# Queries and keys transposed unsplit, and scores as half-height products of two heads

## The chip, the core and the metric

The kernel runs on one core of a Trainium2 chip. The metric is the device time of one execution in microseconds (us), the median of several runs. The engines are named as in the profile: PE (matmul; PEld is its weight load), DVE (vector), ACT (scalar), POOL (GpSimd) and SP, whose queue issues every transfer here.

## The reference

Windowed attention with a distance bias, then a feed-forward layer with a rational activation. All is float32. Sizes: 4 batches, 8 heads, 768 positions, 64 dimensions a head; 8 global and 96 local positions; the feed-forward layer has 3072 tokens, 512 by 2048 weights.

```python
scores = scale * np.matmul(q, k.transpose(0, 1, 3, 2))
is_global = pos[None, :] < int(n_global)
is_local = (rel >= 0) & (rel < int(n_local))
keep = is_global | is_local
scores = scores + bias[None, :, :, :]          # -slope of the head * distance
scores = np.where(keep, scores, -1000000000.0)
a = np.exp(scores - np.max(scores, axis=-1, keepdims=True))
a = a / (np.sum(a, axis=-1, keepdims=True) + 1e-09)
x = np.matmul(a, v)                            # to [3072, 512]
h = x @ w_in
g = (a0 + a1*h + a2*h*h + a3*h*h*h) / (1 + |b0|*|h| + |b1|*h*h + 1e-6)
out = g @ w_out
```

## The kernel before

The 3072 tokens are 24 blocks of 128 positions (i is the block's number in its batch, 0 to 5). A unit u is one block with two neighbouring heads (p is the pair of heads), so there are 96 units; two units that follow each other share a load of q, k and v for four heads. Here m = u // 2 numbers these. A chunk is two blocks, 256 tokens: 8 units of attention and 8 steps f of the feed-forward layer.

The float32 products run in one of two ways. In one, a number is split into a high part, rounded to the type float32r (`FR`), and the low rest, and a product becomes three products of these parts of float32r operands; in the other it stays one product of plain float32 operands. The feed-forward layer after the first chunk goes the first way, with weights and activations split: `st_ffn1` (line 257, output `h`, 256 columns) and `st_ffn2` (line 333, output `acc`, 512 columns). In the first chunk both run on plain float32 (lines 249 and 328), while the weights are still being loaded, decoded (lines 162 to 191; some bit work on DVE, ACT and POOL) and split (lines 208, 209).

Attention, for one unit, in stages:

- `st_load` (lines 131 to 134): three transfers bring q and k of four heads into `nat`, v into `vt`.
- `st_split` (368, 369): DVE rounds q and k of two heads to float32r, POOL subtracts to get the low part; both lie side by side in `sp`, 64 columns high and 64 low for each head.
- `st_qkT` (377): four transposes on PE. For each head the result `tk` has the 64 high rows above the 64 low rows.
- `st_qkE` (391 to 396): ACT brings q (times a power of two that belongs to the head) into `qT` and k into `kT`. Two transfers on SP (392, 393) make a second copy of q in which the high and low halves of the partitions have changed places. `kT` keeps two blocks of keys per head, the block's own and the one before; `kG` keeps the first 8 keys, which line 409 copies into the older block.
- `st_score` (407, output `s`): two products per head over all 128 rows, one with `qT` and one with the exchanged copy, so that all four products of high and low parts are summed. DVE (418) adds the mask, scales and takes the minimum of each row.
- `st_soft` (428 to 433): ACT takes the exponential, DVE adds up and inverts. `st_norm` (440): POOL scales the probabilities.
- `st_pT` (450, output `tp`): PE transposes the probabilities. For each pair of units, `st_pv` (467, output `o`) multiplies with v, each head into 64 of the 128 output columns, and `st_x` (486, 487) splits the result into `xh` and `xl` for the feed-forward layer.

PSUM has two buffers for `h`, two for `acc`, one for the activation and three, tagged `t`, that `tk`, `s`, `tp` and `o` share in turn.

One loop over t calls all stages; each call gets a priority from t and a table (`PRI`, `PRI_A` for the first chunk), and a scheduler orders the instructions of every engine from these priorities and from its own simulated timeline. Attention runs 12 units ahead of the feed-forward layer (`LAG`). Each engine then takes its own instructions in that fixed order, and so does the queue of SP.

A second path for other window sizes (`general`) is compiled in, but with these inputs it isn't taken.

Of the kernel before, what the change touches and what calls it, by code (L numbers as in the profile page):

```python
# [94 lines left out]
def tile_kernel(ctx: ExitStack, tc: tile.TileContext, q, k, v, n_global, n_local,  # L95
# [126 lines left out]
    stats = const.tile([P, 4, 8], F32, name="stats")  # L222

    def load_coef():
        nc.sync.dma_start(out=coef[:, 0:4], in_=ca.partition_broadcast(P))
# [122 lines left out]
    ident = const.tile([P, P], F32, name="ident")  # L350
# [13 lines left out]
    def st_split(u):
        p = unit(u)[2]
        n = nat[u // 2][:, :, 2 * (p % 2):2 * (p % 2) + 2, :]
        s = pl.att.tile([P, 2, 2, 2, D], FR, tag="split", name=f"sp{u}", bufs=1)
        nc.vector.tensor_copy(out=s[:, :, :, 0, :], in_=n)  # L368
        nc.gpsimd.tensor_tensor(out=s[:, :, :, 1, :], in0=n, in1=s[:, :, :, 0, :], op=ALU.subtract)  # L369
        sp[u] = s  # L370

    def st_qkT(u):
        s = sp.pop(u)
        tk = pl.ps_t.tile([P, 2, 2, P], FR, tag="t", name=f"tk{u}")
        for z in range(2):
            for x in range(2):
                nc.tensor.transpose(out=tk[:, z, x, :], in_=s[:, z, x].rearrange("p a d -> p (a d)"),  # L377
                                    identity=ident_r)
        tqk[u] = tk

    def st_qkE(u):
        c, t, p, b, i = unit(u)
        tk = tqk.pop(u)
        hs = slice(2 * p, 2 * p + 2)
        qT = pl.att.tile([P, 2, 2, P], FR, tag="qT", name=f"qT{u}", bufs=3)
        for x in range(2):

            nc.scalar.activation(out=qT[:, 0, x], in_=tk[:, 0, x], func=AF.Copy, scale=float(2.0 ** (2 * p + x - 2)))
        nc.sync.dma_start(out=qT[0:D, 1].bitcast(F32), in_=qT[D:P, 0].bitcast(F32))
        nc.sync.dma_start(out=qT[D:P, 1].bitcast(F32), in_=qT[0:D, 0].bitcast(F32))
        nc.scalar.copy(out=kT[:, hs, i % 2, :], in_=tk[:, 1])
        if i == 0:
            nc.scalar.copy(out=kG[:, hs, :], in_=tk[:, 1, :, 0:G])
        qTs[u] = qT

    def st_score(u):
        c, t, p, b, i = unit(u)  # L400
        qT = qTs.pop(u)
        s_ps = pl.ps_t.tile([P, 2, 2, P], F32, tag="t", name=f"s{u}")
        for x in range(2):
            h = 2 * p + x
            rhs = kT[:, h] if i else kT[:, h, 0:1, :].broadcast_to([P, 2, P])
            for z in range(2):
                nc.tensor.matmul(out=s_ps[:, x], lhsT=qT[:, z, x, :], rhs=rhs, start=(z == 0), stop=(z == 1))  # L407
        if 1 <= i < NT - 1:
            nc.gpsimd.tensor_copy(out=kT[:, 2 * p:2 * p + 2, i % 2, 0:G], in_=kG[:, 2 * p:2 * p + 2, :])
        if i == 0:  # L410
            mk = mask0
        else:
            mk = masks[:, 0:2, :] if i % 2 else masks[:, 1:3, :]
        pr = pl.att.tile([P, 2, 2, P], F32, tag="prob", name=f"pr{u}")
        st = stats[:, u % 4]
        for x in range(2):
            h = 2 * p + x
            nc.vector.tensor_tensor_reduce(  # L418
                out=blocks_of(pr[:, x], i), in0=blocks_of(s_ps[:, x], i), in1=mk,
                scale=-(2.0 ** -(h + 1)), scalar=3e38, op0=ALU.add, op1=ALU.min, accum_out=st[:, x:x + 1])  # L420
        prob[u] = (pr, st)

    def st_soft(u):
        i = unit(u)[4]
        pr, st = prob[u]
        for x in range(2):
            d = blocks_of(pr[:, x], i)
            nc.scalar.activation(out=d, in_=d, func=AF.Exp, scale=-1.0, bias=st[:, x:x + 1],  # L428
                                 accum_out=st[:, 2 + 2 * x:3 + 2 * x])

        nc.vector.tensor_reduce(out=st[:, 6:8], in_=st[:, 2:6].rearrange("p (x w) -> p x w", w=2), op=ALU.add,
                                axis=mybir.AxisListType.X)
        nc.vector.reciprocal(out=st[:, 6:8], in_=st[:, 6:8])  # L433

    def st_norm(u):
        i = unit(u)[4]
        pr, st = prob[u]
        for x in range(2):
            d = blocks_of(pr[:, x], i)
            nc.gpsimd.tensor_scalar(  # L440
                out=d, in0=d, scalar1=st[:, 6 + x:7 + x], scalar2=None, op0=ALU.mult)
# [51 lines left out]
    def windowed():  # L493
# [217 lines left out]
```

## Time and profile before

| | |
|---|---|
| median of 3 runs | 793.19 us (793.1 to 794.15) |
| the profiled execution | 793.47 us, of which its span is 791.7 us |
| busy, PE / PEld | 745.0 us (94%) / 647.2 us (82%) |
| busy, DVE / ACT / POOL | 589.6 us (74%) / 573.0 us (72%) / 531.7 us (67%) |
| matmuls | 5184 records |
| granted PE clock, mean | 0.996 |

The span runs from the first to the last instruction. In the rows of the profile a name like `s<-kT,qT` is output and inputs by the program's names, `L407` the line, `128*64 128x128` the part of the array used (rows by columns of weights) and the size of the output. A plain float32 product with no transpose leaves two records in the trace. Rows of matmuls overlap, since they are pipelined: what one costs the next is the distance between their starts. A group's row ends with the idle time of its engine ahead of it and what ended that. Stretches are given in us from the start of the span.

### The profile page before, as it was taken

The numbers are of one execution on the slowest core, as the hardware profiler recorded it, in microseconds if no ns is written. First come the engines' busy times: TensorE is split into PE (matmuls) and PEld (weight loads), VectorE is DVE, ScalarE is ACT, GpSimd is POOL, SyncE is SP. The second block draws the span as 40 slices with busy tenths as digits, with TensorE's granted clock in tenths as the row PEclk, the third lists the DMA queues.
The fourth block names the chain that finished last, engine by engine and source line by source line (L and its number), as shares of the span: only waits on it lengthen the run. The fifth ranks groups of instructions, "written<-read, shape, count | busy, mean of one in ns | idle before, by whom it ended". The sixth has DMA issues, their size and how long they took to land.

```text
span 791.7 us, 15480 instructions
## 1 busy us (share of the span) xinstructions
PE 745.0 (94%) x5184; PEld 647.2 (82%) x5184; DVE 589.6 (74%) x1453; ACT 573.0 (72%) x1407; POOL 531.7 (67%) x572
## 2 busy tenths in 40 slices
PE   3678998899999999999999999999999999999995
PEld 2466656598988998988998988988998988988993
DVE  5899998988786767776776767776776767776664
ACT  4688767776786777777777777777777777776763
POOL 3887657998966676675676676675677676664440
PEclk9999999999999999999999999999999999999999
DMA  7884555122121222222222222222222222100000
GB/s 182 233 228 144 158 156 159 44 65 64 43 58 23 62 55 49 62 54 58 57 47 49 61 55 48 61 55 53 63 48 48 61 56 48 41 15 1 27 1 32
DMA packets 101400, 55.90 MB, mean 71 GB/s; under 512 B 81856, under 2 KB 94144, under 8 KB 101312
## 3 DMA queue, kind: packets, MB, share of 16 engines
q1 hardware_dynamic: 101312, 54.82, 26.3%
q8 instruction: 44, 0.72, 0.4%
q14 instruction: 44, 0.36, 0.1%
HBM read 35.92 MB, written 6.29 MB: 53 GB/s over the span
## 4 chain that ended last, share of the span: by engine, by line
PE 81%; DVE 9%; POOL 3%; DMA 2%; issue 2%; ACT 1%; SPq 0%; DVEq 0%; POOLq 0%; ACTq 0%
PE h L257 32%; PE acc L333 30%; PE s L407 5%; PE o L467 5%; PE tp L450 4%; PE tk L377 3%; POOL pr L440 2%; PE acc L328 1%; DMA qT<-qT 1%; DVE pr L418 1%; DMA r<-in_moe_w_out_dram 1%; DVE fu L304 1%; POOL sp L369 1%; DVE fu L288 1%; DVE r L189 1%
## 5 line engine op out<-in xcount | busy, mean ns | idle before, releaser
L333 PE MATMUL acc<-wout_h,g 128*128 128x512 f32 x704 | 250.1, 406 | 0.8 <-ACT g L312 0.8
L257 PE MATMUL h<-xh,win_h 128*128 128x256 f32 x704 | 204.7, 291 | 2.4 <-DVE fu L289 2.4
L440 POOL TENSOR_SCALAR pr<-pr,stats 128x256 f32<-128x256 f32 (+1 forms) x192 | 180.5, 950 | 32.9 <-DVE stats L433 15.5
L257 PE MATMUL h<-xl,win_h 128*128 128x256 f32 x704 | 197.7, 281 | 0.0
L290 POOL TENSOR_TENSOR fa<-fa,fs 128x512 f32<-128x512 f32 x95 | 124.5, 1311 | 91.1 <-ACT fs L283 87.3
L333 PEld LDWEIGHTS acc<-wout_h,g 128*128 128x128 f32 x704 | 128.5, 188 | 23.3 <-ACT g L312 1.2
L257 PEld LDWEIGHTS h<-xh,win_h 128*128 128x128 f32 x704 | 132.5, 188 | 11.3 <-issue 6.6
L369 POOL TENSOR_TENSOR sp<-nat,sp 128x256 fp32r<-128x256 f32 x96 | 75.9, 791 | 95.8 <-DVE sp L368 45.8
L257 PEld LDWEIGHTS h<-xl,win_h 128*128 128x128 f32 x704 | 132.4, 188 | 1.8 <-issue 0.5
L428 ACT ACTIVATE pr<-pr,stats 128x256 f32<-128x256 f32 (+1 forms) x192 | 92.6, 485 | 55.2 <-DVE stats L418 55.0
L281 ACT ACTIVATE fu<-h,coef 128x512 f32<-128x512 f32 (+1 forms) x97 | 75.0, 774 | 60.3 <-PE h L257 59.4
L313 POOL TENSOR_TENSOR g<-fu,g 128x512 fp32r<-128x512 f32 x87 | 112.7, 1295 | 7.9 <-DVE fu L289 4.5
L302 DVE SCALAR_TENSOR_TENSOR fu<-fu,coef,q 128x512 f32<-128x512 f32 (+1 forms) x97 | 71.6, 738 | 48.2 <-ACT q L298 47.2
L297 ACT ACTIVATE fs<-fa,coef 128x512 f32<-128x512 f32 (+1 forms) x97 | 69.6, 718 | 34.9 <-POOL fa L290 32.5
L452 DVE COPY pT<-tp 128x512 f32<-128x512 f32 (+1 forms) x75 | 48.5, 646 | 61.8 <-PE tp L450 61.2
L288 DVE TENSOR_TENSOR fu<-fu,h 128x512 f32<-128x512 f32 (+1 forms) x97 | 65.3, 673 | 12.3 <-ACT fs L283 10.7
L407 PE MATMUL s<-kT,qT 128*128 128x256 f32 x384 | 70.2, 304 | 4.4 <-DMA qT<-qT 3.4
L289 DVE SCALAR_TENSOR_TENSOR fu<-fu,coef,h 128x512 f32<-128x512 f32 (+1 forms) x97 | 71.8, 740 | 2.6
L450 PE MATMUL tp<-ident,pr 128*128 128x128 f32 x352 | 63.0, 282 | 10.7 <-POOL pr L440 10.2
L303 DVE SCALAR_TENSOR_TENSOR q<-fa,coef,q 128x512 f32<-128x512 f32 (+1 forms) x97 | 72.1, 743 | 0.0
L407 PEld LDWEIGHTS s<-kT,qT 128*128 128x128 f32 x384 | 60.4, 199 | 11.6 <-issue 2.4
L283 ACT ACTIVATE fs<-h,coef 128x512 f32<-128x512 f32 (+1 forms) x97 | 66.5, 685 | 0.1
(271 smaller groups left out, 1622.5 us busy)
## 6 DMA issues: line engine op xcount, KB each, us to landing
qT<-qT SPq DMA_DIRECT2D x192, 64.0 KB, 2.1
r<-in_moe_w_in_dram SPq DMA_DIRECT2D x16, 512.0 KB, 5.4
r<-in_moe_w_out_dram SPq DMA_DIRECT2D x16, 512.0 KB, 3.5
nat<-in_q_dram SPq DMA_DIRECT2D x48, 128.0 KB, 2.7
nat<-in_k_dram SPq DMA_DIRECT2D x48, 128.0 KB, 2.5
vt<-in_v_dram SPq DMA_DIRECT2D x48, 128.0 KB, 2.3
out_dram<-o SPq DMA_DIRECT2D x24, 256.0 KB, 2.1
vt<-in_v_dram SPq DMA_DIRECT2D x32, 8.0 KB
```

What stands on the lines that cost most here:

```text
L257: nc.tensor.matmul(out=hps[f][:, y, :], lhsT=w[:, fs], rhs=x[:, ct, :], start=(n == 0), stop=(n == 3 * NCT - 1))
L281: nc.scalar.activation(out=u, in_=h, func=AF.Identity, scale=a3, bias=a2)
L288: nc.vector.tensor_tensor(out=u, in0=u, in1=h, op=ALU.mult)
L290: side(f).tensor_tensor(out=a, in0=a, in1=s, op=ALU.add)
L303: nc.vector.scalar_tensor_tensor(out=r, in0=a, scalar=q1, in1=r, op0=ALU.add, op1=ALU.mult)
L313: side(f).tensor_tensor(out=g[:, 1, ys], in0=u, in1=g[:, 0, ys], op=ALU.subtract)
L333: nc.tensor.matmul(out=acc, lhsT=gs[f][:, z, y, ts], rhs=w, start=(ft == 0 and n == 0), stop=(ft == NFT - 1 and n == 2))
L369: nc.gpsimd.tensor_tensor(out=s[:, :, :, 1, :], in0=n, in1=s[:, :, :, 0, :], op=ALU.subtract)
L407: nc.tensor.matmul(out=s_ps[:, x], lhsT=qT[:, z, x, :], rhs=rhs, start=(z == 0), stop=(z == 1))
L428: nc.scalar.activation(out=d, in_=d, func=AF.Exp, scale=-1.0, bias=st[:, x:x + 1], accum_out=st[:, 2 + 2 * x:3 + 2 * x])
L440: nc.gpsimd.tensor_scalar(out=d, in0=d, scalar1=st[:, 6 + x:7 + x], scalar2=None, op0=ALU.mult)
L450: nc.tensor.transpose(out=t_ps[:, x, w, :], in_=pr[:, x, w, :], identity=ident)
```

## The change

q and k are no longer split ahead of the transposes. They are loaded into a new tile `natf`, and a transfer within SBUF copies them to `nat`, which has the type float32r: the bits stay as they are, without rounding. PE transposes these for two pairs of heads at once: `tk` of one m holds q of both pairs and k of both pairs, where a pair's two heads have 64 rows each. The split is made on the way out of PSUM: ACT rounds to the high parts, DVE subtracts to get the low parts. `qT` and `kT` now hold high and low parts in separate planes, with one head of a pair in rows 0 to 63 and the other in rows 64 to 127; the exchanged copy and its two transfers are gone. A score is three products (high by high, high by low, low by high) over 64 rows; the two heads of a pair write two different `t` buffers, and the source issues their products in turn. `qkT`, `qkE`, `score` and `soft` run once per m, on all four heads; the first eight keys are copied by POOL.

```diff
-        n = pl.ldp.tile([P, 2, 4, D], F32, tag="nat", name=f"nat{u}")
-        nc.sync.dma_start(out=n[:, 0], in_=q[b, hs, r, :].rearrange("h s d -> s h d"))
-        nc.sync.dma_start(out=n[:, 1], in_=k[b, hs, r, :].rearrange("h s d -> s h d"))
+        nf = pl.ldp.tile([P, 2, 4, D], F32, tag="natf", name=f"natf{u}", bufs=1)
+        n = pl.ldp.tile([P, 2, 4, D], FR, tag="nat", name=f"nat{u}")
+        nc.sync.dma_start(out=nf[:, 0], in_=q[b, hs, r, :].rearrange("h s d -> s h d"))
+        nc.sync.dma_start(out=nf[:, 1], in_=k[b, hs, r, :].rearrange("h s d -> s h d"))
+        nc.sync.dma_start(out=n.bitcast(F32), in_=nf)
...
+    def st_qkT(m):
+        n = nat[m]
+        tk = pl.ps_t.tile([P, 2, 2, P], FR, tag="t", name=f"tk{m}")
         for z in range(2):
+            for y in range(2):
+                nc.tensor.transpose(out=tk[:, z, y, :], in_=n[:, z, 2 * y:2 * y + 2, :].rearrange("p a d -> p (a d)"),
+                                    identity=ident_r)
+        tqk[m] = tk.bitcast(F32)
+
+    def st_qkE(m):
+        p, i = of_pairs(m)
+        tk = tqk.pop(m)
+        qT = qTs[m] = pl.att.tile([P, 2, 2, P], FR, tag="qT", name=f"qT{m}")
+        kh, kl = (kT[:, p:p + 2, z, i % 2, :] for z in range(2))
+        for y in range(2):
+            nc.scalar.activation(out=qT[:, 0, y], in_=tk[:, 0, y], func=AF.Identity, scale=qs[:, p + y:p + y + 1])
+        nc.scalar.copy(out=kh, in_=tk[:, 1])
+        for y in range(2):
+            nc.vector.scalar_tensor_tensor(out=qT[:, 1, y], in0=tk[:, 0, y], scalar=qs[:, p + y:p + y + 1],
+                                           in1=qT[:, 0, y], op0=ALU.mult, op1=ALU.subtract)
+        nc.vector.tensor_tensor(out=kl, in0=tk[:, 1], in1=kh, op=ALU.subtract)
+        if i == 0:
+            nc.gpsimd.tensor_copy(out=kG[:, p:p + 2], in_=kT[:, p:p + 2, :, 0, 0:G])
+
+    def st_score(m):
+        p, i = of_pairs(m)
+        qT = qTs.pop(m)
+        sx = [pl.ps_t.tile([P, 2, 2, P], F32, tag="t", name=f"s{x}_{m}") for x in range(2)]
+        for y in range(2):
+            for n, (zq, zk) in enumerate(((0, 0), (0, 1), (1, 0))):
+                for x in range(2):
+                    r = slice(x * D, (x + 1) * D)
+                    nc.tensor.matmul(out=blocks_of(sx[x][:, y], i), lhsT=qT[r, zq, y, :],
+                                     rhs=blocks_of(kT[r, p + y, zk], i), start=(n == 0), stop=(n == 2))
...
-            on("score", st_score, t - 2)
-            on("soft", st_soft, t - 2)
+                on_m("score", st_score, m - 1)
+                on_m("soft", st_soft, m - 1)
             on("ffn1a", st_ffn1, f, 0)
-            on("qkT", st_qkT, t)
-            if t % 2:
-                on("pv", lambda u: st_pv(u // 2), t - 5)
-            on("qkE", st_qkE, t)
-            if t % 2:
-                on("x", lambda u: st_x(u // 2), t - 5)
-            if t:
-                on("split", st_split, t + 1)
+            if odd:
+                on_m("qkT", st_qkT, m)
+                on_m("pv", st_pv, m - 2)
+                on_m("qkE", st_qkE, m)
+                on_m("x", st_x, m - 2)
```

More of the change, by code (lines that the diff above doesn't have):

```diff
@@ L221, in tile_kernel @@
     a0, a1, a2, a3, b0, _, b1, q1 = (coef[:, x:x + 1] for x in range(8))
-    stats = const.tile([P, 4, 8], F32, name="stats")
+    stats = const.tile([P, 4, 16], F32, name="stats")
     def load_coef():
@@ L342, in st_ffn2 @@
             nc.sync.dma_start(out=out[rows, :], in_=o)
-    kT = const.tile([P, H, 2, P], FR, name="kT")
-    kG = const.tile([P, H, G], FR, name="kG")
+    kT = const.tile([P, NPAIR, 2, 2, P], FR, name="kT")
+    kG = const.tile([P, NPAIR, 2, G], FR, name="kG")
     ident = const.tile([P, P], F32, name="ident")
     ident_r = const.tile([P, P], FR, name="ident_r")
+    qs = const.tile([P, NPAIR], F32, name="qs")
     mask0 = const.tile([P, P], F32, name="mask0")
     masks = const.tile([P, 3, P], F32, name="masks")
-    sp = {}
+    qTs = {}
     tqk = {}
-    qTs = {}
     prob = {}
@@ L362, in blocks_of @@
         return x if i else x[..., 0, :]
[L364 to L374, printed above, removed]
-        for z in range(2):
-            for x in range(2):
-                nc.tensor.transpose(out=tk[:, z, x, :], in_=s[:, z, x].rearrange("p a d -> p (a d)"),
-                                    identity=ident_r)
-        tqk[u] = tk
@@ L384, in st_qkE @@
[L384 to L388, printed above, removed]
-        for x in range(2):
[L391 to L441, printed above, removed]
+    def of_pairs(m):
+        c, t, p, b, i = unit(2 * m)
+        return p, i
+    def st_qkT(m):
+        n = nat[m]
+        tk = pl.ps_t.tile([P, 2, 2, P], FR, tag="t", name=f"tk{m}")
+        for z in range(2):
+            for y in range(2):
+                nc.tensor.transpose(out=tk[:, z, y, :], in_=n[:, z, 2 * y:2 * y + 2, :].rearrange("p a d -> p (a d)"),
+                                    identity=ident_r)
+        tqk[m] = tk.bitcast(F32)
@@ new lines, in st_score @@
+    def st_score(m):
[8 more added lines that the diff above has]
+                                     rhs=blocks_of(kT[r, p + y, zk], i), start=(n == 0), stop=(n == 2))
+        if 1 <= i < NT - 1:
+            nc.gpsimd.tensor_copy(out=kT[:, p:p + 2, :, i % 2, 0:G], in_=kG[:, p:p + 2])
+        mk = mask0 if i == 0 else masks[:, 0:2, :] if i % 2 else masks[:, 1:3, :]
+        st = stats[:, m % 4]
+        for y in range(2):
+            u = 2 * m + y
+            prob[u] = pl.att.tile([P, 2, 2, P], F32, tag="prob", name=f"pr{u}", bufs=3)
+            for x in range(2):
+                nc.vector.tensor_tensor_reduce(
+                    out=blocks_of(prob[u][:, x], i), in0=blocks_of(sx[x][:, y], i), in1=mk,
+                    scale=-(2.0 ** -(2 * (p + y) + x + 1)), scalar=3e38, op0=ALU.add, op1=ALU.min,
+                    accum_out=st[:, 2 * y + x:2 * y + x + 1])
@@ new lines, in st_soft @@
+    def st_soft(m):
+        i = of_pairs(m)[1]
+        st = stats[:, m % 4]
+        for n in range(4):
+            d = blocks_of(prob[2 * m + n // 2][:, n % 2], i)
+            nc.scalar.activation(out=d, in_=d, func=AF.Exp, scale=-1.0, bias=st[:, n:n + 1],
+                                 accum_out=st[:, 4 + 2 * n:5 + 2 * n])
+        nc.vector.tensor_reduce(out=st[:, 12:16], in_=st[:, 4:12].rearrange("p (x w) -> p x w", w=2), op=ALU.add,
+                                axis=mybir.AxisListType.X)
+        nc.vector.reciprocal(out=st[:, 12:16], in_=st[:, 12:16])
@@ L443, in st_pT, with st_norm @@
+    def st_norm(u):
+        m, y = divmod(u, 2)
+        i = of_pairs(m)[1]
+        for x in range(2):
+            d = blocks_of(prob[u][:, x], i)
+            nc.gpsimd.tensor_scalar(out=d, in0=d, scalar1=stats[:, m % 4, 12 + 2 * y + x:13 + 2 * y + x],
+                                    scalar2=None, op0=ALU.mult)
     def st_pT(u):
         i = unit(u)[4]
-        pr, st = prob.pop(u)
+        pr = prob.pop(u)
         W = 2 if i else 1
@@ L499, in windowed @@
         nc.vector.tensor_copy(out=ident_r, in_=ident)
+        for p in range(NPAIR):
+            for x in range(2):
+                nc.gpsimd.memset(qs[x * D:(x + 1) * D, p:p + 1], 2.0 ** (2 * p + x - 2))
         nc.vector.tensor_copy(out=nf, in_=ni)
         load_coef()
-        st_split(0)
-        st_split(1)
         nl, ng = nf[:, 0:1], nf[:, 2:3]
```

7 lines of the change are left out of this document (6 added, 1 removed).

## The prediction

> **What bounds the kernel now.** I read the busy time by stretch first, then who waits for whom on TensorE, then single stretches of its timeline, then the groups by line, and the chain of the opening last. The four stretches (columns: window, length, then busy time and instructions of PE, PEld, DVE, ACT, POOL, granted clock, DMA share, GB/s):
>
> ```profile
> 0.00:20.00 20.00, 7.04 (x34) 5.82 (x34) 11.52 (x59) 9.13 (x35) 6.94 (x18) 1.00 0.73 184
> 20.00:160.00 140.00, 116.23 (x649) 82.87 (x649) 131.78 (x323) 105.57 (x272) 107.87 (x108) 0.99 0.56 161
> 160.00:740.00 580.00, 579.44 (x4256) 522.02 (x4255) 417.99 (x1027) 429.09 (x1051) 400.28 (x435) 1.00 0.20 49
> 740.00:791.70 51.70, 42.31 (x251) 36.52 (x249) 28.31 (x47) 29.24 (x52) 16.59 (x13) 0.97 0.06 23
> ```
>
> From 160 to 740 us PE is covered for 579.44 of 580 us, while DVE, ACT and POOL are at 69 to 74%. Before that, DVE is the full one: 131.78 of 140 us. Cover alone does not prove that PE sets the pace, since each matmul's row includes its way through the pipe; its waits do, from 160 us on:
>
> ```profile
> PE h L257 <- DVE fu L289: 1.8, 1, 1.8
> PE acc L333 <- ACT g L312: 0.8, 1, 0.8
> PE s L407 <- ACT kT L394: 0.6, 1, 0.6
> ```
>
> So 3.2 us of waits in 630. In this stretch a step added to PE's queue is a step added to the time, and work taken from DVE, ACT or POOL is worth nothing. I therefore cost PE by start-to-start steps, not by durations. The timeline of PE (start, length, instruction) at one block of four transposes `tk`:
>
> ```profile
> 407.56 0.28 PE L257 MATMUL h<-xh,w_2l 128*128 128x256 f32 x1
> 407.68 0.46 PE L377 MATMUL tk<-ident_r,sp 128*128 128x128 f32 x4
> 407.98 0.35 PE L257 MATMUL h<-xh,win_h 128*128 128x256 f32 x1
> 408.16 0.29 PE L257 MATMUL h<-xl,win_h 128*128 128x256 f32 x1
> ```
>
> A 256-column product steps by 0.12 us (407.56 to 407.68; a row further down gives 0.118). The block and the product behind it take 408.16 - 407.68 = 0.48 us, so the block costs 0.36 us. Four scores, next:
>
> ```profile
> 404.14 0.66 PE L407 MATMUL s<-kT,qT 128*128 128x256 f32 x4
> 404.63 0.40 PE L333 MATMUL acc<-wout_h,g 128*128 128x512 f32 x1
> ```
>
> 0.49 us, some 0.12 each. Then `o` (L467), the only products here that do not use the whole array (128 rows by 64 columns, the two heads alternating), in a run of 16 records and one of 8; each of its products leaves two records:
>
> ```profile
> 712.10 0.28 PE L257 MATMUL h<-xh,w_2l 128*128 128x256 f32 x1
> 712.31 1.09 PE L467 MATMUL o<-pT,vt 128*64 128x128 f32 x16
> 713.33 0.38 PE L257 MATMUL h<-xh,win_h 128*128 128x256 f32 x1
> 713.55 0.28 PE L257 MATMUL h<-xl,win_h 128*128 128x256 f32 x1
> ...
> 714.73 0.28 PE L257 MATMUL h<-xh,w_2l 128*128 128x256 f32 x1
> ...
> 386.31 0.66 PE L467 MATMUL o<-pT,vt 128*64 128x128 f32 x8
> 386.89 0.38 PE L257 MATMUL h<-xh,win_h 128*128 128x256 f32 x1
> ...
> 95.79 3.69 PE L249 MATMUL h<-x,w_2f 128*128 128x256 f32 x16
> 99.41 0.43 PE L467 MATMUL o<-pT,vt 128*64 128x128 f32 x2
> ```
>
> From 713.55 to 714.73 are ten L257 steps: 0.118 each. Eight more records of `o` take (713.33 - 712.31) - (386.89 - 386.31) = 0.44 us, 0.055 each. L249, of the same type and on the whole array, takes (99.41 - 95.79) / 16 = 0.226 us for 256 columns, 0.113 for 128: twice as much, so in `o` two halves of the array run side by side. But there is a fixed price. From 712.10 to 713.55 are 1.45 us; two L257 steps (0.236) and 16 records (0.88) leave 0.33 to 0.34 us. Of it 0.09 shows ahead of the run (712.10 to 712.31), 0.10 behind the first product after it (713.33 to 713.55), the rest inside. One run of `o` thus costs 0.34 us beyond its work.
>
> **What the order does.** An m is two units, that is, four heads of one 128-row block. The names: `s` score, `tk` transposed q and k, `o` output of attention, `tp` transposed probabilities, `acc` and `h` the two FFN products. PE at the scores, before (one unit):
>
> ```order
> L333 MATMUL acc_1_6563<-wout_h,g_6442 128x512 x2
> L333 MATMUL acc_1_6563<-w_1l,g_6442 128x512
> L333 MATMUL acc_1_6563<-wout_h,g_6442 128x512
> L407 MATMUL s_6570<-kT,qT_6403 128x256 x4
> L257 MATMUL h_6582<-xh_5603,win_h 128x256
> ```
>
> PE at the scores of m = 30, now (`s_30_5284` is the first head of each pair, rows 0 to 63; `s_30_5285` the second, rows 64 to 127):
>
> ```order
> L448 MATMUL tp_5261<-ident,pr_5105 128x128 x4
> L407 MATMUL s_30_5284<-kT,qT_5209 128x256 x6
> L335 MATMUL acc_0_4609<-wout_h,g_5058 128x512 x2
> L335 MATMUL acc_0_4609<-w_13l,g_5058 128x512
> L335 MATMUL acc_0_4609<-wout_h,g_5058 128x512
> L335 MATMUL acc_1_4621<-wout_h,g_5058 128x512 x2
> L335 MATMUL acc_1_4621<-w_13l,g_5058 128x512
> L335 MATMUL acc_1_4621<-wout_h,g_5058 128x512
> L407 MATMUL s_30_5285<-kT,qT_5209 128x256 x6
> ```
>
> The source writes the two heads in turn, but the six products of one stand apart from the six of the other: the second score tile gets its PSUM buffer later. PE at `o`, before:
>
> ```order
> L377 MATMUL tk_6595<-ident_r,sp_6514 128x128 x4
> L467 MATMUL o_6600<-pT_6462,vt_5670 64x128 x2
> L467 MATMUL o_6600<-pT_6462,vt_5264 64x128 x2
> L467 MATMUL o_6600<-pT_6561,vt_5670 64x128 x2
> L467 MATMUL o_6600<-pT_6561,vt_5264 64x128 x2
> L257 MATMUL h_6582<-xh_5603,win_h 128x256
> ```
>
> and now:
>
> ```order
> L378 MATMUL tk_5576<-ident_r,nat_5084 128x128 x4
> L465 MATMUL o_5581<-pT_5457,vt_4716 64x128 x2
> L465 MATMUL o_5581<-pT_5457,vt_4351 64x128 x2
> L259 MATMUL h_5563<-xh_4471,win_h 128x256
> L259 MATMUL h_5563<-xl_4472,win_h 128x256
> L259 MATMUL h_5563<-xh_4471,w_0_2l 128x256
> L259 MATMUL h_5563<-xh_4471,win_h 128x256
> L259 MATMUL h_5563<-xl_4472,win_h 128x256
> L465 MATMUL o_5581<-pT_5555,vt_4716 64x128 x2
> L465 MATMUL o_5581<-pT_5555,vt_4351 64x128 x2
> ```
>
> One run of `o` has become two. The trace of before starts its matmuls in the compiled order. Counted over it from the first split FFN product on (near 160 us): before, 37.5 m with 300 scores, 43 runs of `o`; now 39 m with 468 scores in 68 runs, 78 runs of `o`. Of the 468, 72 have 128 columns, and 67 stand right behind one of the other head without a partner yet. I take 38 m for the full stretch.
>
> **The sum, PE, per m.**
> 1. Transposes: one block of four instead of two. -0.36.
> 2. Scores: 12 products instead of 8. At 0.118 each, 1.42 against 0.94. The 128-column ones step by 0.07 (a `tk` block has four in 0.30), which saves 1.85 x 0.05 = 0.09; partners side by side, as in `o`, save 1.7 x 0.11 = 0.19. Net +0.19. Without any overlap it is +0.38.
> 3. Runs of `o`: 2.0 instead of 1.15, at 0.34. +0.29.
> 4. Runs of half-height products: 1.74, where there were none. No row shows one. The lower bound is 0. The upper is the price of `o`, 0.34, with a full weight load in place of a half one at both edges, 0.05 each (rows below: 188 against 136 ns): 0.44. Nearest is `o`, also a product on part of the array; I add the wider load at the entry alone: 0.39. +0.68.
>
> ```profile
> L407 PEld LDWEIGHTS s<-kT,qT 128*128 128x128 f32 x291 | 44.1, 188 | 6.0 <-ACT kT L394 0.8
> L467 PEld LDWEIGHTS o<-pT,vt 128*64 128x64 f32 x560 | 30.3, 136 | 3.8 <-issue 0.6
> ```
>
> Ends: +4 with term 4 at 0, +40 with 0.44 and no overlap in term 2. Together +0.80 us per m, times 38: +30. Term 4 is 26 of it. The Trainium skill, page "TensorEngine Tiling (Array Packing)", section "Tiling Modes", says that a change of tiling mode, not merely of tile, drains TensorE. The rows of `o` agree for columns (0.34 us a run); no run here shows rows yet. By that rule the sum is the +30 above; without it, +4.
>
> **The other engines, per m.** Their rows from 160 to 740 us:
>
> ```profile
> L369 POOL TENSOR_TENSOR sp<-nat,sp 128x256 fp32r<-128x256 f32 x71 | 52.6, 740 | 77.7 <-DVE stats L431 33.8 <-DVE sp L368 33.3 <-DVE stats L433 6.6
> L368 DVE CAST sp<-nat 128x256 fp32r<-128x256 f32 x70 | 25.5, 365 | 34.8 <-POOL kT L409 13.7 <-PE tk L377 8.9 <-POOL g L313 7.1
> L487 DVE TENSOR_TENSOR xl<-o,xh 128x256 fp32r<-128x256 f32 x38 | 15.9, 417 | 3.1 <-ACT xh L486 3.1
> L418 DVE CUSTOM_DVE_ANT_0 pr<-s,mask 128x128 f32<-128x128 f32 x24 | 6.0, 284 | 0.2
> L433 DVE RECIPROCAL stats<-stats 128x2 f32<-128x2 f32 x73 | 11.6, 159 | 1.0
> L431 DVE TENSOR_REDUCE stats<-stats 128x2 f32<-128x4 f32 x73 | 11.1, 152 | 10.1 <-ACT pr L428 10.0
> L391 ACT ACTIVATE qT<-tk 128x128 fp32r<-128x128 f32 x144 | 30.4, 262 | 3.0 <-PE tk L377 2.9
> L394 ACT CAST kT<-tk 128x256 fp32r<-128x256 f32 x72 | 26.6, 369 | 0.0
> ```
>
> POOL loses two subtractions, -1.48 us. ACT loses half of its evictions, 2 x 262 + 369, -0.89. DVE loses two casts (0.73) and one pair of reduce and reciprocal (0.31); it gains three subtractions out of PSUM, 2 x 0.284 + 0.417 by the nearest rows: -0.05. POOL has eight small fills more at the start. In the full stretch all of this is slack.
>
> On SP, four transfers of the two halves of `qT` go and one inside SBUF comes, which waits for both loads and for the transposes of the m two earlier; behind it stand the loads of v and the stores of results. `qT` took 2.1 us to land (issue row: `qT<-qT`, 64 KB). The data are wanted two m later, some 28 us, so I cost it at nothing there. At the very start nothing covers it.
>
> The opening, to 165 us, by the chain of what ended last:
>
> ```profile
> by line: issue 8.6%; POOL pr L440 7.4%; PE acc L328 6.7%; DMA qT<-qT 3.7%; DVE pr L418 3.7%; DMA r<-in_moe_w_out_dram 3.6%; PE h L257 3.4%; POOL sp L369 3.1%; DVE r L189 3.0%; DMA r<-in_moe_w_in_dram 3.0%; PE s L407 3.0%; PE tk L377 2.8%; D
> ```
>
> `qT` and `sp`, which go, are 6.8% of 165 us: 11 us at most. The low end is -11. The high end is +5, two landings in a row before the first transposes. DVE, nearly full there, hardly loses work, so I take -4.
>
> The profiled execution took 793.5 us, against the median of 793.2: 793.5 + 30 - 4 = 820 us.
>
> **The rivals.**
> - *Half-height runs cost nothing* (term 4 is 0). For it: the scores keep all 128 columns, and the measured price is one of split columns. Against it: in `o` the price sits at both edges, as a pipe that empties would. 794 us with my opening, 787 with its low end. This is the case on the faster side: it ends below 791.6 if a run costs under 0.07 us and the opening gives its 11.
> - *PSUM buffers become the wait.* Scores now hold two of the three `t` buffers at once, and `tk`, `tp` and `o` need the third. For it: the heads torn apart above. Against it: of the PE waits above at most the 0.6 us of `s` for ACT can be a `t` buffer, and tiles per m fall from 7 to 6. At half a us per m: +19, 839 us.
> - *Weight loads within a half no longer hide.* Each of the 8.6 products per m without a partner of the other half would add its 0.188: +61, 881 us. Against it: L407 loads 0.188 us for every 0.118 step on one set of rows. The Trainium skill, "TensorE: Matmul & The Clock Gate", Part 3, says that weight loads overlap running matmuls only when the row group differs; those rows contradict it for the full array.
>
> **How the numbers follow.** 0.68 for 820, 0.20 for free runs, 0.07 for PSUM, 0.05 for weight loads. A measurement here can tell about 0.2%, 1.6 us. Free runs split into 0.10 faster, 0.05 same, 0.05 slower; the rest is slower: 0.85. The range leaves out about a tenth below (free runs with a short opening) and the weight loads with half of the PSUM case above: 792 to 842.
>
> **What would show it.** `tk` rows halve to 192. The L407 rows read 64*128. At the edges of their runs PE steps some 0.2 us, as at `o`; if they step 0.12, term 4 is wrong. Inside a run of one head steps stay at 0.12, and a pair of two heads starts within 0.01 us. Between 160 us and the last score PE stays covered, with waits of a few us; waits of `s`, `tk` or `tp` for DVE or ACT of over 10 us mean the PSUM rival. POOL's busy time falls by some 70 us, without use.

## The result, and the profile after

The changed kernel takes 829.05 us (median of 4 runs, 826.8 to 830.16), the kernel before 793.67 us on the same chip (4 runs): ratio 1.044, interval 1.0414 to 1.0467. The profiled execution took 829.64 us, its span is 827.8 us: 36.1 us more than before. The prediction said 820 us, between 792 and 842.

Busy time by stretch (columns as in the prediction; the last stretch again begins some 52 us ahead of the end):

```profile
0.00:20.00 20.00, 3.72 (x21) 2.74 (x21) 10.79 (x57) 8.14 (x24) 5.11 (x22) 1.00 0.71 202
20.00:160.00 140.00, 114.99 (x585) 79.68 (x586) 123.63 (x289) 90.55 (x218) 80.41 (x78) 0.94 0.51 154
160.00:776.00 616.00, 615.33 (x4330) 527.59 (x4329) 426.18 (x1016) 423.19 (x955) 345.97 (x349) 1.00 0.17 47
776.00:827.80 51.80, 42.56 (x252) 36.78 (x250) 28.57 (x47) 29.52 (x52) 16.60 (x13) 0.97 0.07 23
```

PE is covered for 615.33 of 616 us, and the other engines have become emptier. Who PE waits for from 160 us on:

```profile
PE h L259 <- DVE fu L291: 1.8, 1, 1.8
PE acc L335 <- ACT g L314: 0.8, 1, 0.8
PE s L407 <- ACT pT L450: 0.7, 1, 0.7
```

3.3 us, as before. So the time of the full stretch lies in PE's own steps. Its timeline at two runs of six scores (one head each), then at a run of twelve (the heads in turn):

```profile
550.39 0.40 PE L335 MATMUL acc<-w_2l,g 128*128 128x512 f32 x1
550.72 0.97 PE L407 MATMUL s<-kT,qT 64*128 64x256 f32 x6
551.62 0.39 PE L259 MATMUL h<-xh,win_h 128*128 128x256 f32 x1
551.84 0.28 PE L259 MATMUL h<-xl,win_h 128*128 128x256 f32 x1
552.05 0.97 PE L407 MATMUL s<-kT,qT 64*128 64x256 f32 x6
552.95 0.39 PE L259 MATMUL h<-xh,w_2l 128*128 128x256 f32 x1
553.17 0.28 PE L259 MATMUL h<-xh,win_h 128*128 128x256 f32 x1
...
441.39 0.28 PE L259 MATMUL h<-xh,win_h 128*128 128x256 f32 x1
441.60 0.99 PE L407 MATMUL s<-kT,qT 64*128 64x256 f32 x12
442.51 0.39 PE L259 MATMUL h<-xl,win_h 128*128 128x256 f32 x1
442.74 0.28 PE L259 MATMUL h<-xh,w_3l 128*128 128x256 f32 x1
```

Into the second run the step is 0.21 us (551.84 to 552.05), out of it 0.22 (552.95 to 553.17), where `h` steps by 0.118 elsewhere. From 551.84 to 553.17 are 1.33 us; less two steps of `h` (0.236) that is 1.09 us for six products, whose own steps are 6 x 0.118 = 0.71: one run costs 0.39 us beyond its work (the median of ten such runs with `h` on both sides is 1.098 us). The run of twelve takes 442.74 - 441.39 - 0.236 = 1.11 us: twelve products of two heads in turn cost what six of one head do.

The instructions by line, over the whole span:

```profile
L407 PE MATMUL s<-kT,qT 64*128 64x256 f32 x480 | 61.1, 307 | 0.7 <-ACT pT L450 0.7
L407 PE MATMUL s<-kT,qT 64*128 64x128 f32 x96 | 14.2, 319 | 1.7 <-ACT kT L389 1.0 <-DVE fl L669 0.6
L378 PE MATMUL tk<-ident_r,nat 128*128 128x128 f32 x192 | 26.0, 261 | 21.2 <-DMA nat<-natf 9.3 <-DVE scr L77 7.9 <-DVE stats L417 2.2
```

The transposes are half as many (192), and in the opening they wait: 9.3 us for the transfer inside SBUF, 7.9 us at the very first. The opening's chain to 90 us:

```profile
by line: DMA nat<-natf 20.4%; DMA natf<-in_k_dram 17.1%; DMA r<-in_moe_w_in_dram 10.2%; issue 5.6%; DMA r<-in_moe_w_out_dram 4.6%; PE h L251 4.2%; DVE pr L417 2.9%; SPq L132 2.2%; DVE w_7f L179 1.9%; DVE w_6f L177 1.9%; PE s L407 1.7%; DVE 
```

Load of q and k, transfer into `nat`, next load: through the one buffer `natf` they stand in a row and are 37.5% of it.

**An account of PE's time.** For this kernel and each experiment I add up the start-to-start times of PE's records, from the first transposes on, in three parts. *Steps*: each record at the step that it has inside a run (`h` 0.118, `acc` 0.231, `tp` 0.108, `tk` 0.07, a score of 256 columns 0.118 and of 128 columns the forecast's 0.07, a record of `o` 0.055, plain float32 `h` 0.215 us; a score whose partner of the other head starts within 0.03 us counts nothing). *Runs*: 0.39 us for each run of half-height scores, 0.34 for each run of `o`. *Rest*: what is left, that is waits and steps longer than these (the plain float32 `acc` of the first chunk among them). With the start of the first transposes and some 7 us behind PE's last start this makes up the span.

| kernel (ratio to before) | first start | steps | runs of scores, of `o` | runs, us | rest to 180 us | 180 to 740 us | later |
|---|---|---|---|---|---|---|---|
| before | 5.0 | 684.2 | none half-height, 57 | 19.4 | 64.9 | 7.8 | 3.3 |
| changed (1.044) | 7.9 | 673.4 | 80, 87 | 60.8 | 68.1 | 6.9 | 3.7 |
| e_full_rows (1.025) | 8.1 | 688.8 | none half-height, 86 | 29.3 | 67.0 | 7.7 | 3.9 |
| e_one_run_o (1.045) | 8.1 | 674.8 | 85, 60 | 53.6 | 72.6 | 7.5 | 4.2 |
| e_reuse_s (1.010) | 7.7 | 658.2 | 63, 70 | 48.4 | 72.7 | 4.9 | 3.9 |
| e_reuse_late (1.013) | 7.6 | 658.0 | 61, 63 | 45.2 | 74.7 | 9.8 | 3.3 |
| e_two12 (1.047) | 7.5 | 673.5 | 83, 87 | 61.9 | 68.5 | 7.2 | 3.5 |
| e_pool_open (1.044) | 5.0 | 673.4 | 79, 88 | 60.8 | 70.7 | 6.8 | 4.5 |
| e_o_later (1.035) | 7.8 | 662.3 | 85, 56 | 52.2 | 74.1 | 12.3 | 3.7 |
| e_join (1.066) | 7.6 | 660.6 | 51, 50 | 36.9 | 89.5 | 37.1 | 5.8 |
| e_join_pool (1.062) | 4.9 | 661.1 | 53, 51 | 38.0 | 93.8 | 28.7 | 5.6 |
| e_join_full (1.077) | 7.8 | 688.8 | none half-height, 50 | 17.0 | 91.5 | 36.6 | 7.0 |
| e_join_lag13 (1.040) | 7.8 | 662.0 | 52, 51 | 37.6 | 86.2 | 19.9 | 3.6 |
| e_join_lag14 (1.040) | 7.9 | 661.9 | 50, 50 | 36.5 | 82.7 | 22.8 | 4.2 |

From before to the changed kernel: steps -10.8, runs +41.4, rest +2.7, start +2.9: +36.2 us. The 0.07 is too little: in the trace a score of 128 columns with no partner beside it steps by 0.112 us. The changed kernel has 84 of these, so some 3.5 us of its rest are steps; the kernel before has none.

### The profile page after: what moved, and what is told of

Read it like the earlier page. It is cut to its first block, busy times and chain, and to the rows that moved or that the text cites. A ratio compares the mean times of both kernels' runs of the same rounds, so it can differ in the third digit from the quotient of the medians.

```text
span 827.8 us, 14633 instructions
## 1 busy us (share of the span) xinstructions
PE 776.6 (94%) x5184; PEld 646.8 (78%) x5184; DVE 589.2 (71%) x1406; ACT 551.4 (67%) x1246; POOL 448.1 (54%) x460
## 4 chain that ended last, share of the span: by engine, by line
PE 84%; DVE 7%; DMA 6%; issue 1%; ACT 1%; SPq 0%; POOL 0%; POOLq 0%; ACTq 0%
PE h L259 33%; PE acc L335 30%; PE s L407 7%; PE o L465 6%; PE tp L448 4%; DMA nat<-natf 2%; PE acc L330 2%; DMA natf<-in_k_dram 2%; PE tk L378 1%; DMA r<-in_moe_w_in_dram 1%; PE h L251 1%; DVE pr L417 1%; DVE q L305 1%; DVE fu L290 1%; DMA r<-in_moe_w_out_dram 0%
## 5 line engine op out<-in xcount | busy, mean ns | idle before, releaser
L335 PE MATMUL acc<-wout_h,g 128*128 128x512 f32 x704 | 240.2, 403 | 0.8 <-ACT g L314 0.8
L438 POOL TENSOR_SCALAR pr<-pr,stats 128x256 f32<-128x256 f32 (+1 forms) x192 | 173.3, 919 | 101.6 <-DVE stats L431 57.7
L259 PE MATMUL h<-xl,win_h 128*128 128x256 f32 x704 | 200.0, 284 | 0.0
L335 PEld LDWEIGHTS acc<-wout_h,g 128*128 128x128 f32 x704 | 126.8, 188 | 25.6 <-issue 2.2
L407 PE MATMUL s<-kT,qT 64*128 64x256 f32 (+1 forms) x576 | 75.4, 309 | 2.4 <-ACT kT L389 1.0
L407 PEld LDWEIGHTS s<-kT,qT 64*128 64x128 f32 x576 | 59.4, 199 | 21.3 <-issue 10.4
L417 DVE CUSTOM_DVE_ANT_0 pr<-s,masks 128x256 f32<-128x256 f32 x160 | 60.4, 420 | 21.4 <-PE s L407 20.9
L448 PE MATMUL tp<-ident,pr 128*128 128x128 f32 x352 | 60.6, 285 | 13.3 <-POOL pr L438 7.3
L314 ACT CAST g<-fu 128x512 fp32r<-128x512 f32 (+1 forms) x89 | 55.2, 620 | 19.6 <-DVE fu L306 19.5
```

Source lines behind the costliest of these rows:

```text
L259: nc.tensor.matmul(out=hps[f][:, y, :], lhsT=w[:, fs], rhs=x[:, ct, :], start=(n == 0), stop=(n == 3 * NCT - 1))
L335: nc.tensor.matmul(out=acc, lhsT=gs[f][:, z, y, ts], rhs=w, start=(ft == 0 and n == 0), stop=(ft == NFT - 1 and n == 2))
L407: nc.tensor.matmul(out=blocks_of(sx[x][:, y], i), lhsT=qT[r, zq, y, :], rhs=blocks_of(kT[r, p + y, zk], i), start=(n == 0), stop=(n == 2))
L438: nc.gpsimd.tensor_scalar(out=d, in0=d, scalar1=stats[:, m % 4, 12 + 2 * y + x:13 + 2 * y + x], scalar2=None, op0=ALU.mult)
```

## The experiments

The first takes the price of the score runs away, the second joins the runs of `o`, the third fills the score runs up with both heads; the fourth, and e_pool_open further down, ask about the opening. The e_join group asks whether fewer runs of both kinds give a kernel that beats the one before. All ratios are to the kernel before on the same chip (795.23, 794.91 and 794.46 us in the three groups of runs).

**e_full_rows**

```diff
-                    r = slice(x * D, (x + 1) * D)
+                    r = slice(0, P)
```

> The score products take all 128 rows instead of 64 (each then sums two heads, so the separation of the heads is left out); nothing else changes, and the number of products, of rows in PSUM and of runs (65 instead of 68) stays. Theory, a fixed price of 0.39 us for each run of half-height products on TensorE: 68 x 0.39 = 26.5 us go, while the 67 products that had run beside one of the other head now take a step of their own (67 x 0.11 = +7 us): 829 - 26.5 + 7 = 810 us, and the step into and out of a run of scores falls from 0.21 to 0.12 us. Rival, the full stretch is longer through waits for PSUM buffers or other engines: these are as before, so 829 us or, with the lost overlap, 836. The milestones of the opening (+9 us at the 97th split FFN product) stay with both.

814.51 us, ratio 1.0248 (1.0216 to 1.028): 15 us less than the changed kernel. PE's timeline at its scores:

```profile
506.19 0.28 PE L259 MATMUL h<-xh,win_h 128*128 128x256 f32 x1
506.31 1.46 PE L407 MATMUL s<-kT,qT 128*128 128x256 f32 x11
507.61 0.62 PE L335 MATMUL acc<-wout_h,g 128*128 128x512 f32 x2
```

The step into the run is 0.12 us, and 11 products take 1.30 us, 0.118 each: on the whole array the run has no price. The 80 runs of the whole program are worth 31 us; the lost partners cost 15, twice what I expected, since the trace of the changed kernel has 135 partners over the whole program and I had counted 67 in the order of the full stretch. The waits rival is out. One part of the expectation missed: the 97th split FFN product, which I use as a mark for the end of the opening, did not stay at 176.8 us but came at 169.6. The 18 runs of scores ahead of it in the changed kernel are worth 7.0 us at 0.39 each. The Trainium skill, page "TensorEngine Tiling (Array Packing)", section "Tiling Modes", says that a change of tiling mode drains TensorE and a change of tile does not. This run and the run of twelve above agree with both halves, and put 0.39 us on it.

**e_one_run_o**

```diff
-        for y in range(2):
+        for y in (1, 0):
...
+                    if (y, n, x) != (1, 0, 0):
+                        tc.keep_in_program_order(ins)
```

> The eight products of one attention output are kept in one piece in TensorE's queue. Runs of `o` in the full stretch fall from 78 to 53, runs of scores rise from 68 to 72. Theory, a run costs its fixed price wherever it stands: -25 x 0.34 + 4 x 0.39 = -7 us, 822 us. Rival, what a run costs is only moved (the products wait for the last of their transposed probabilities while the rest of the queue stands behind them): 829 us or more, with waits of `o` for ACT or DVE in the place of the runs.

830.95 us, 1.0453 (1.0436 to 1.0471): no gain. The account has the runs 7.2 us cheaper, as expected, and the rest up to 180 us 4.5 us longer. PE's waits up to 180 us, of which the changed kernel had 1.1 us for `fu` and none for `o`:

```profile
PE acc L330 <- DVE fu L306: 7.2, 5, 2.4
PE o L465 <- ACT pT L450: 5.1, 4, 2.1
```

The saved runs paid for waits in the opening: there `o` now needs the younger probabilities first, and what is behind it in PE's queue is late too.

**e_reuse_s**

```diff
-        sx = [pl.ps_t.tile([P, 2, 2, P], F32, tag="t", name=f"s{x}_{m}") for x in range(2)]
+        sx = [tks.pop(m), pl.ps_t.tile([P, 2, 2, P], F32, tag="t", name=f"s1_{m}")]
...
-                for x in range(2):
+                for x in (1, 0):
...
+                    if (y, n, x) != (0, 0, 1):
+                        tc.keep_in_program_order(ins)
```

> The score tile of the first head takes over the PSUM buffer of the transposes `tk` of the same m, and the twelve products stand in turn, head by head, in one piece of TensorE's queue. Runs of scores fall from 68 to some 49, steps of scores from 401 to 234 (every product beside its partner), runs of `o` from 78 to 62. Theory: -19 x 0.39 - 167 x 0.11 - 16 x 0.34 = -7 - 18 - 5 = -30 us, 799 us; a run of twelve takes 1.11 us in all, no more than a run of six. Rival 1, half-height products of two heads do not gain from the neighbour (the pairs seen in the trace are only starts, and the weight loads still take their turn): -7 - 5 = 817 us. Rival 2, the buffer held longer makes `tk` or the scores wait: 829 us or more, with waits of TensorE of over 10 us for ACT or DVE.

803.86 us, 1.0104 (1.0083 to 1.0125): 27 us less than the changed kernel by the ratios (0.0336 x 795), the best of the changed forms. PE's timeline at one m (the products into the shared buffer read `tk`):

```profile
444.12 0.28 PE L259 MATMUL h<-xh,win_h 128*128 128x256 f32 x1
444.33 0.38 PE L408 MATMUL s<-kT,qT 64*128 64x256 f32 x1
444.33 0.39 PE L408 MATMUL tk<-kT,qT 64*128 64x256 f32 x1
444.55 0.28 PE L408 MATMUL s<-kT,qT 64*128 64x256 f32 x1
444.56 0.28 PE L408 MATMUL tk<-kT,qT 64*128 64x256 f32 x1
...
445.02 0.27 PE L408 MATMUL s<-kT,qT 64*128 64x256 f32 x1
445.03 0.28 PE L408 MATMUL tk<-kT,qT 64*128 64x256 f32 x1
445.23 0.38 PE L259 MATMUL h<-xl,win_h 128*128 128x256 f32 x1
445.45 0.28 PE L259 MATMUL h<-xh,w_0l 128*128 128x256 f32 x1
```

The two heads start within 0.01 us of each other, pair by pair, and one m costs 445.45 - 444.12 - 0.236 = 1.09 us in all. Rival 1 is out, and so is rival 2 (829 us or more). Against the changed kernel the account has steps -15.2 and runs -12.4 us; up to 180 us 4.6 us of it go to the rest.

**e_two12**

```diff
-        nf = pl.ldp.tile([P, 2, 4, D], F32, tag="natf", name=f"natf{u}", bufs=1)
+        if u % 4 and u < 12:
+            nf = tmp(f"natf{u}").rearrange("p a (b d) -> p a b d", d=D)
+        else:
+            nf = pl.ldp.tile([P, 2, 4, D], F32, tag="natf", name=f"natf{u}", bufs=1)
```

> Up to the sixth pair of units every second one stages q and k in a second buffer (taken from another pool), so that the next load need not wait for the copy inside SBUF of the one before. Runs in the full stretch are 67 and 78, as in the changed kernel. Theory, the opening is long because load, copy and next load stand in one chain through the single buffer `natf` (34 us of the opening's chain): the 97th split FFN product comes at 171 instead of 176.8 us, 823 us in all. Rival 1, SP is held by the wait for the tile `nat` (27 us for the transposes two m earlier) and by the copy's own time, not by the staging buffer: 828 us. Rival 2, the opening is bound by DVE and the loads come early enough: 829 us.

831.82 us, 1.047 (1.0448 to 1.0492): no gain. The 97th `h` product on split operands (the 97th split FFN product of the expectation) comes at 177.6 us, in the changed kernel at 176.8. In the chain to 90 us loads and transfers of q and k fell from 37.5% to 11.6%, and the weights' transfers rose from 14.8% to 23.2%. My theory of the opening fails here. The loads came off the chain and the end stood still, so they were early enough, as rival 2 has it; that DVE binds the opening is not shown, and by the time alone the rivals (828 and 829 us) can't be told apart.

**e_join** (the shared buffer as in e_reuse_s, for m of 9 and more, with head 0 first; the products of an `o` kept in their order; priorities 60 and 70 for `pv` and `x`; and:)

```diff
                 on_m("score", st_score, m - 1)
+                on_m("pv", st_pv, m - 3)
+                on_m("x", st_x, m - 3)
                 on_m("soft", st_soft, m - 1)
...
             if odd:
+                on("pT", st_pT, t - 3)
                 on_m("qkT", st_qkT, m)
-                on_m("pv", st_pv, m - 2)
                 on_m("qkE", st_qkE, m)
-                on_m("x", st_x, m - 2)
...
-            on("pT", st_pT, t - 3)
+            if not odd:
+                on("pT", st_pT, t - 3)
```

> The output product of an m is written into the program one step later, directly behind the scores, its eight products are kept in one order, the transposes of the probabilities come ahead of `tk`, and from m = 9 on the score tile of head 0 takes over the buffer of `tk`. In TensorE's queue the full stretch then holds 40 runs of scores (68 in the changed kernel), 235 steps of scores (401) and 41 runs of `o` (78); the opening is ordered nearly as it was. Theory, price per run: -28 x 0.39 - 166 x 0.11 - 37 x 0.34 = -11 - 18 - 13 = -42 us: 788 us, under the kernel before. Rival, keeping products together only turns runs into waits, as the one run of `o` did: 800 to 804 us, as with the shared buffer alone, and TensorE's time beyond steps and runs grows by over 8 us.

846.99 us, 1.0656 (1.0628 to 1.0684): 59 us above the expectation. The runs went as counted (51 and 50, 36.9 us), but the rest grew by 54 us. PE's timeline where the feed-forward layer goes over to the next chunk, and PE's waits from 180 to 740 us:

```profile
299.18 0.40 PE L335 MATMUL acc<-wout_h,g 128*128 128x512 f32 x1
299.41 0.40 PE L259 MATMUL h<-xh,win_h 128*128 128x256 f32 x2
...
303.55 0.28 PE L259 MATMUL h<-xh,w_0l 128*128 128x256 f32 x1
...
304.06 0.52 PE L451 MATMUL tp<-ident,pr 128*128 128x128 f32 x3
305.45 0.36 PE L259 MATMUL h<-xh,win_h 128*128 128x256 f32 x1 [0.86 <-DVE fu L291]
```

```profile
PE h L259 <- DVE fu L291: 19.1, 20, 1.6
```

The last `o` of a chunk now comes one step later, the step in which the next chunk's `h` is wanted. By then the old chunk's `acc` are done; PE fills both buffers of `h` in one piece and then has nothing until DVE has emptied one. These waits are 19.1 of the 30 us by which the rest of this stretch grew; 21 us more lie ahead of 180 us.

**e_join_pool** (e_join, and `nc.gpsimd.tensor_copy(out=n, in_=nf)` in the place of the transfer)

> As e_join, but q and k go from the staging buffer into the float32r tile by a copy on POOL instead of the transfer inside SBUF (the copy rounds q and k, so their low parts are zero; the number of products stays). Runs in the full stretch are 42 and 41 instead of 40 and 41. Theory, the transfer is late only in the opening, where it costs some 6 us (2.9 at the first transposes, 3 to 180 us) and nothing later, where POOL has slack for the copies: 782 us, and the first transposes start near 5 us instead of 7.9. Rival 1, another chain of the opening (the weights' loads and their decoding on DVE) is as long: 788 us, with the first transposes early all the same. Rival 2, the transfers inside SBUF also cost the full stretch: under 778 us.

843.12 us, 1.0616 (1.0592 to 1.0639): 4 us less than e_join. The first transposes start at 4.9 instead of 7.6 us, yet the 97th split FFN product comes at 192.1 us, in e_join at 192.2: rival 1 for the opening. The gain lies in the full stretch, whose rest is 8 us smaller. On so disturbed a base I take no more from it.

**e_join_full** (e_join with `r = slice(0, P)`)

> As e_join, with all 128 rows in each score product (each sums two heads, so the separation of the heads is left out). Theory: 51 runs of half-height products over the whole program lose their price, -51 x 0.39 = -20 us, and 285 products lose the partner beside which they ran, 285 x 0.11 = +31 us: 11 us longer than e_join, 799 us; here half-height products pay, since a run holds twelve of them. Rival, the price is not one per run but one per product or per change of head: full rows are then faster, by 10 us or more, as they were in the changed kernel.

856.57 us, 1.0774 (1.0747 to 1.0801): 9.4 us longer than e_join (0.0118 x 795), against 11 expected. The same edit that saved 15 us in the changed kernel costs 9 here: where a run holds both heads, half-height products earn more than the run's price.

**e_o_later** (of e_join only the place of `st_pv` and `st_x` behind the scores, and the order of the eight products)

> Of e_join only the place of the output product in the program (one step later, directly behind the scores) and the fixed order of its eight products; the scores are as in the changed kernel. This alone takes the full stretch from 401 to 258 steps of scores (the two heads stand together again, since the second score tile gets its buffer in time) and from 78 to 46 runs of `o`, with 69 runs of scores. Theory: -143 x 0.11 - 32 x 0.34 = -16 - 11 = -27 us: 802 us. Rival, the one run of `o` turns into waits as it did without the later place: some 812 us, with the 16 us of the scores alone.

821.97 us, 1.0346 (1.0321 to 1.0371): 7 us less than the changed kernel instead of 27. Steps and runs fell by 11.1 and 8.6 us, and the rest took back 11.4 us, half of it in the full stretch, as in e_join.

**e_join_lag13, e_join_lag14** (e_join with `LAG = 13` and `LAG = 14`)

> As e_join, with the FFN of a unit written into the program 13 instead of 12 steps behind its attention, so that the last `o` of a chunk again stands a step ahead of the first FFN product that reads it. 42 runs of scores, 237 steps, 42 runs of `o` in the full stretch. Theory, e_join lost its 54 us because at each chunk of eight units the queue ran out of other products before the new chunk's input was there (from 299.4 to 305.4 us only `h` of the new chunk, then a wait for DVE): beyond steps and runs TensorE spends some 80 us again instead of 132, 795 us. Rival, DVE's longer chain (evictions of `tp` ahead of the FFN's) is what `h` waits for, at any lag: 840 us or more.

> As e_join_lag13 with 14 steps: 39 runs of scores, 234 steps, 41 runs of `o`. Theory: some 2 us less in the full stretch, the opening about 0 to 4 us longer since the FFN starts later: 793 to 799 us. Rival as there: 840 us or more.

826.08 us, 1.0402 (1.0379 to 1.0426), and 825.39 us, 1.0396 (1.0368 to 1.0424). One step of lead takes back 21 of the 54 us, two no more: between theory and rival. The rest from 180 to 740 us fell from 37.1 to 19.9 us, where 7 would be as before, and the opening's stayed long (86.2 and 82.7). PE's longest waits up to 180 us in e_join_lag13:

```profile
PE tp L451 <- POOL pr L441: 18.3, 7, 7.2
PE o L468 <- DVE stats L420: 11.0, 4, 4.3
```

In the changed kernel the first of these is 7.3 us, and the second does not occur. Why POOL and DVE are late there, I did not find.

**e_pool_open**

```diff
-        nc.sync.dma_start(out=n.bitcast(F32), in_=nf)
+        if u < 8:
+            nc.gpsimd.tensor_copy(out=n, in_=nf)
+        else:
+            nc.sync.dma_start(out=n.bitcast(F32), in_=nf)
```

> The changed kernel, where the first eight units' q and k (four m, the transfers that stand in the opening's chain at 4.2, 11.0, 21.8 and 30.3 us) go into the float32r tile by a copy on POOL, which rounds them; all later ones by the transfer. Runs in the full stretch stay (66 and 79, 401 steps). Theory, the late q and k are the opening's loss of 6 us: 823 us, the first transposes start near 5 us, and TensorE's time beyond steps and runs up to 180 us falls from 68 to 65 us. Rival, another chain (weights' loads and their decoding) is as long: 829 us, although the transposes are early.

829.97 us, 1.0442 (1.0416 to 1.0468): no gain. Its first transposes and scores, then those of the changed kernel, then its chain to 90 us:

```profile
4.99 0.75 PE L381 MATMUL tk<-ident_r,nat 128*128 128x128 f32 x4 [4.99 <-POOL nat L135]
11.38 0.47 PE L410 MATMUL s<-kT,qT 64*128 64x128 f32 x2 [5.64 <-ACT kT L392]
```

```profile
7.88 0.72 PE L378 MATMUL tk<-ident_r,nat 128*128 128x128 f32 x4 [7.88 <-DVE scr L77]
9.65 0.48 PE L407 MATMUL s<-kT,qT 64*128 64x128 f32 x2 [1.04 <-ACT kT L389]
```

```profile
by line: DMA r<-in_moe_w_in_dram 14.0%; PE h L254 13.2%; DMA r<-in_moe_w_out_dram 10.0%; issue 6.8%; DMA coef<-in_moe_b_dram 6.6%; POOL pr L441 5.9%; ACT pr L430 3.3%; DVE pr L420 2.4%; ACT w_2f L175 2.0%; DVE r L194 1.7%; DVE fu L294 1.5%;
```

The transposes are as early as before the change (5.0 us), the 97th split FFN product comes at 174.7 instead of 176.8 us, and the transfers are gone from the chain; the first scores wait 5.6 us for ACT instead and come at 11.4 us, and loads and decoding of the weights fill the chain. First start and rest to 180 us add up to 75.7 us; 76.0 in the changed kernel, 76.0 with two buffers, 69.9 before.

**e_reuse_late**

```diff
-                for x in range(2):
+                for x in ((1, 0) if m >= 4 else (0, 1)):
...
-        for y in range(2):
+        for y in ((1, 0) if m >= 6 else (0, 1)):
```

> The shared buffer of e_reuse_s from m = 4 on, and from m = 6 on the eight products of an `o` kept in one order at their old place. 51 runs of scores, 240 steps, 55 runs of `o` (50, 242 and 62 in e_reuse_s). Theory: -7 x 0.34 = -2 us in the full stretch, and the 4.6 us that e_reuse_s lost up to 180 us come back for the most part: 798 us. Rival, the waits of `o` for its probabilities eat the saved runs: 804 us.

805.62 us, 1.0128 (1.0106 to 1.015): not less than e_reuse_s. Runs fell by 3.2 us, the rest rose by 6.3. No form that I tried beats the kernel before.

## Why the prediction was right, and where it was not

- **PE sets the full stretch.** Right: 615.33 of 616 us covered, waits of 3.3 us. POOL's busy time fell by 83.6 us (531.7 to 448.1), forecast as some 70, without any use.
- **Runs of half-height products (term 4).** Right in mechanism and, for 256 columns, in size: 0.39 us assumed and measured. 62 runs on 36 m from 180 to 740 us are 1.72 per m (1.74 forecast). e_full_rows shows the cause by taking it away, e_reuse_s by filling the runs. The rival of free runs is out. The reason given for 0.05 of the price, the wider weight load, is not borne out: runs of 128 columns have weight loads of the same shape and length (0.183 to 0.188 us) and cost 0.33 (rows below). That 0.39 met the mark is in part luck.
- **Runs of `o` (term 3).** 68 runs on 36 m against 40 on 35 in that stretch, that is 1.9 and 1.1 per m; forecast 2.0 and 1.15.
- **Scores (term 2).** Mis-sized twice, in opposite directions. In that stretch 93 partners on 36 m are 2.6 per m, not 1.7 (the other 42 lie in the opening), which saves some 4 us more on 38 m. But products of 128 columns do not step by 0.07, a step taken from the transposes:

```profile
398.86 0.28 PE L259 MATMUL h<-xh,win_h 128*128 128x256 f32 x1
399.06 0.88 PE L407 MATMUL s<-kT,qT 64*128 64x128 f32 x6
399.88 0.39 PE L259 MATMUL h<-xl,win_h 128*128 128x256 f32 x1
400.10 0.28 PE L259 MATMUL h<-xh,w_0l 128*128 128x256 f32 x1
```

Six of them take 400.10 - 398.86 - 0.236 = 1.00 us, little less than six of 256 columns (1.10); inside the run they step by 0.112, which leaves 0.33 for the price. So the 0.09 us per m was a saving of 0.01, and some 3 us are missing. That the two nearly cancel is luck.
- **PSUM and weight loads.** Neither rival occurred: 0.7 us of waits of scores, and the products of one head step by 0.118 us in their run of six, where the rival added a weight load of 0.188 to each.
- **The full stretch.** +30 us forecast. From the 97th split FFN product (168.1 us before, 176.8 after) to the end the growth is 36.2 - 8.7 = 27.5 us.
- **The opening.** This is the step that failed: -4 us (from -11 to +5), measured +8.7 at that product. By the account up to that product: start +2.9, rest +3.5, runs +6.4 (18 of scores and 14 of `o` cost 11.8 us; before, 16 of `o` 5.4) and steps -4.1. I had priced the opening by the shares of its chain, as if `qT` and `sp` could go out of it and nothing took their place, and I had let the opening's own runs be covered; e_full_rows, in which the score runs lose their price, has that product at 169.6 us. So the opening was forecast 12.7 us too short and the full stretch 2.5 us too long: 10 us, the whole distance from the sum of 819.5 to the profiled 829.6 us.
- **What the 6 us of start and rest are (6.1 up to 180 us), stays open.** The late q and k are not it alone, though the chain names them: with them early again (e_pool_open), or with a second buffer (e_two12), other waits came up and the end stood still. One thing differs that I did not vary: the granted clock from 20 to 160 us is 0.94, before 0.99. By these figures 115 us of busy PE at 0.05 less would be some 6 us (an estimate). The changed kernel's trace, two stretches (columns as above, the clock third from the end) and PE's timeline:

```profile
57.01:60.42 3.41, 1.24 (x11) 0.65 (x9) 2.41 (x9) 1.64 (x3) 1.38 (x2) 1.00 0.56 173
60.42:70.66 10.24, 8.11 (x33) 6.52 (x34) 8.38 (x20) 6.05 (x18) 6.76 (x5) 0.50 0.72 216
...
65.19 7.27 PE L251 MATMUL h<-x,w_0f 128*128 128x256 f32 x20 [2.13 <-ACT x L481]
72.30 0.60 PE L448 MATMUL tp<-ident,pr 128*128 128x128 f32 x4
```

Twenty records of plain `h` take 72.30 - 65.19 = 7.11 us; at 0.215 they would take 4.3. At the clock of 0.50 they step by 0.427. Up to 180 us, 20 records of `h` began at that clock (13 of these and 7 later) and took 4.1 us longer than at full clock; before the change, none did. The Trainium skill, page "TensorE: Matmul & The Clock Gate", Part 1, says that the clock is held back unless activity releases it. The trace agrees so far as the clock fell behind a stretch in which PE was busy for 1.24 of 3.41 us. Whether the longer steps set the end is not shown. Against it, e_full_rows ran 20 to 160 us at 0.89, with 3.9 us of such longer steps and no longer rest, and in e_join_lag13 and e_join_lag14, whose openings are long, no record of `h` began at half clock. It was not tried by itself.

## What to carry to other kernels

A product on part of the array has a price per run, not per product: here 0.39 us (0.33 at 128 columns), and at 256 columns 0.118 us saved per pair of heads, so a run pays from four pairs on. Before such a change, count in the compiled order how many runs there will be, and whether the partners stand next to each other, since one PSUM buffer that comes late can tear them apart. Regroup products only after asking what else then comes later: the forms that saved most runs lost more in waits. And do not take a chain's share in a stretch with several chains of like length for a gain.

## What the runs showed that I had not expected

Twelve products of 64 rows, two heads in turn, take 1.09 to 1.11 us, no more than six of one head (1.10 us): partners run fully side by side, weight loads of 0.185 us included. And the granted clock fell to 0.68 from 60 to 80 us in the changed kernel, where PE was busy for 14.93 of 20 us; before it was 1.00 there.
